# One fused VectorE step for single-row columns of a triangular inverse, late copies and scales on ScalarE, and a new instruction order, in an RWKV-7 and SwiGLU kernel on one core

## The chip, the cores and the metric

The kernel runs on one core of a Trainium2 chip. The metric is the device time of one execution in microseconds (us). Its engines are named as in the profile: PE (TensorE's matmuls; PEld its weight loads), DVE (VectorE), ACT (ScalarE), POOL (GpSimd) and SP (SyncE, which here only issues DMAs). Each engine works off its own list of instructions in order; semaphores tie them together.

## What is computed

An RWKV-7 recurrence over 768 tokens, for 4 batches x 8 heads with 40 numbers a head, and behind it a gated feed-forward block over the 3072 x 320 result:

```
for t in range(S):                                  # r, k, v, w, a, b: (4, 8, 768, 40)
    y[:, :, t] = einsum('bhd,bhde->bhe', rt, state)
    Sa = einsum('bhde,bhe->bhd', state, at)
    state = state * wt[:, :, None, :] - einsum('bhd,bhe->bhde', Sa, bt)
    state = state + einsum('bhd,bhe->bhde', vt, kt)
...
rms = sqrt(mean(x * x, axis=-1, keepdims=True) + 1e-06)   # x: (3072, 320)
xn = x / rms * rms_g
g = xn @ w_gate                                           # (320, 1536)
out = (g * sigmoid(g) * (xn @ w_val)) @ w_out             # (1536, 320)
```

All is in fp32.

## The kernel before

The tokens are cut into 24 chunks of 32. Within a chunk the recurrence is written as matrix products and one triangular inverse for each of the 32 sequences, so that the state moves from chunk to chunk only.

- `front(c)` (line 714) loads a chunk, turns it with TensorE, and forms the decay products, the gram matrices (blocks "gramk") and the triangular factors LT, level by level (1, 2, 4, 8, 16).
- `inverse(c)` (line 823, chunks 4 to 23) inverts the triangular matrix M of every sequence by forward substitution on DVE. Partition p holds a quarter of the rows of one sequence's inverse, so step i has n = i // 4 + 1 rows and m = 31 - i columns. Each of the 31 steps is two instructions of helper line 505: a product into `tmp`, and a subtraction of `tmp` from `Yi`. Chunks 0 to 3 use `early_inverse` (line 841).
- `main(c)` (line 873) does the recurrence proper: products with the state ("state", "lower"), a scaled copy Xs, a second "lower", the copies into VU, the "update" of the state ST; then the scores, the masked scores As for each level, the level products, the output y, its norm, and the turned and scaled columns xg that the feed-forward block reads.
- `feed(g)` (line 1003) takes two chunks (256 tokens) through the feed-forward weights in six pairs of slices: "h64" and "h" blocks of matmuls, Silu on ACT (tile sg), a product on DVE (hT), and "out" blocks that add up in the PSUM tile po.
- `narrow` (line 1039) recodes the weights once at the start.

Helper lines are what the profile shows: 505 every DVE operation, 525 ACT activations, 528 ACT copies, 531 ACT scales, 544 DMAs, 547 matmuls, 550 transposes, 1079 the filler matmul.

None of this is issued as it is recorded. A planner class records every operation as a piece with its dependences. The text `ORDER` then lists the pieces in the order in which they are issued; a number is the distance from the first piece not yet issued, and a "-" is a filler, a 128 x 128 matmul with the identity into an unused part of po that keeps TensorE occupied (line 1079). `PAIRS` gives each of the short-lived PSUM areas ("rooms") one of three PSUM tiles. So the order on each engine is written out by hand, as it were, and is fixed when the kernel is built.

`EARLY, LATE = 4, 6` (line 23) splits the chunks. For chunks from LATE on, four places of `main` use DVE where the chunks before use ACT:

- line 893: of the four copies of the solved block into VU (32 x 320 each), the two with q = 1 go to DVE;
- line 913: the two half copies of the turned r (64 x 512) go to DVE;
- line 929: the masked scores of level 16 are one DVE product of 128 x 512 instead of two ACT scales of 128 x 256;
- line 997: the scaled columns xg are one DVE product of 128 x 384 instead of three ACT scales of 128 x 128.

Of the kernel before, what the change touches and what calls it, by code (L numbers as in the profile page):

```python
# [17 lines left out]
P = 128  # L18
# [4 lines left out]
EARLY, LATE = 4, 6  # L23
# [10 lines left out]
4 5 6 7 8 9 10 11 - - 46 - - - - 43 53 18 - 316 323 58 - - 61 47 60 525 27 44 - - - - 12 13 14 15 16 17 19 317  # L34
- - 313 315 324 314 333 327 328 - 318 325 - 326 - - 73 339 - 74 85 93 84 - 94 82 83 334 337 - 336 335 338 -
340 349 20 21 22 350 355 23 342 343 24 25 26 - 367 - 354 348 - 352 - 344 345 363 346 365 347 - - 351 75 76 362
353 360 628 397 29 - 443 455 - 452 442 36 32 56 - 48 38 59 54 31 441 35 456 - 636 - 451 444 - 62 453 446 33 -
454 - 37 70 45 - 626 445 - 41 638 356 125 122 - 1 332 331 321 103 322 113 114 329 - 95 86 98 379 359 78 79 364
87 361 374 366 - 376 - 378 - - - - 373 77 357 368 371 377 375 387 372 89 88 358 - 461 - 386 369 383 90 80 -
380 381 465 370 466 384 - - 99 463 464 462 470 341 - 91 471 - - 478 - - 481 482 - 385 467 395 468 477 - - 476  # L40
- 483 493 480 - 389 391 390 - - 104 392 81 394 393 105 123 102 472 490 479 627 633 64 42 50 398 448 34 - 623 -
57 67 624 55 - 459 49 634 460 449 52 65 457 51 635 637 - - 473 - 474 491 - 475 450 - - 625 96 492 - 97 396 494
- - 489 - 504 382 100 487 488 - 484 506 - - 399 400 495 401 - 402 403 503 404 - - - 485 496 405 406 407 500
408 409 - 410 505 - 411 - 412 413 414 415 416 507 417 418 497 419 516 420 421 643 422 423 424 - 499 425 426
427 428 - 106 644 - - 502 501 498 107 108 429 124 320 0 317 90 576 - 132 577 - 328 99 643 645 511 510 - 484 -
113 646 644 509 107 - - - - 506 - 507 - 512 658 - 386 650 651 - 663 467 675 - - - 108 116 - 109 662 428 647
516 517 518 515 131 - 521 114 648 124 522 - 657 508 - - - 652 429 578 567 524 - - 61 870 456 861 860 - 640 66
445 430 69 - 598 871 26 - 28 64 639 630 67 629 110 519 520 434 656 - 653 - 654 661 - 117 660 659 127 128 - 655
580 - 115 - - 674 - - 579 513 664 - - - 432 143 431 433 118 525 526 670 568 125 126 669 133 581 666 134 135
435 436 437 438 569 141 142 140 119 687 129 - 668 673 667 161 152 151 163 - 665 144 527 528 529 136 137 138  # L50
679 530 531 532 533 671 534 535 536 537 147 676 160 130 573 571 572 570 672 682 145 146 684 148 538 680 539
540 541 542 543 544 545 546 547 548 149 549 550 685 551 552 553 - 554 582 583 686 - 574 153 555 575 681 156
677 162 139 801 164 678 586 688 167 157 689 - 589 595 590 - 604 693 154 165 155 690 587 588 596 1 0 962 135
145 144 113 146 134 663 519 661 662 560 136 137 143 612 121 122 660 556 557 555 646 554 712 520 664 665 562
129 138 655 147 148 149 563 131 564 568 565 132 569 - 713 566 832 668 33 - 827 841 826 825 - - 837 521 - 835
669 842 828 836 838 0 830 524 522 523 165 521 164 714 656 658 569 138 653 713 669 670 671 - 672 570 673 149
674 571 - 572 675 676 677 678 525 842 526 847 846 843 845 844 - 848 527 153 154 132 162 665 528 715 163 962
139 679 680 150 140 174 141 681 151 682 859 683 684 685 851 849 858 666 852 863 686 687 688 853 717 719 716
718 155 166 156 857 861 689 854 864 690 855 158 691 860 159 856 169 876 157 - 160 850 862 - 692 - 869 722 720
723 - - 546 764 182 - 152 183 185 173 167 547 726 573 168 875 574 - 721 - 575 729 731 865 1009 1008 - 600 -  # L60
1019 599 1018 1016 576 866 693 888 730 735 867 738 737 694 734 732 193 161 184 577 657 175 727 578 728 736 874
695 696 697 868 698 699 871 - 870 739 186 963 733 170 171 - 966 964 - 176 965 177 - 187 873 188 746 745 178
179 740 952 741 742 743 744 - 877 883 879 882 700 194 - - 579 881 880 747 180 872 887 886 172 195 885 580 748
582 - 878 889 891 581 884 749 750 751 752 753 829 590 589 1010 1020 896 754 892 - 890 1026 1013 1027 205 701
202 203 1021 1012 - 1022 - 1023 702 828 1028 705 703 950 951 755 - - 1011 894 893 838 756 1017 0 725 726 576
15 851 850 577 848 772 16 852 849 855 864 17 714 8 - 9 10 18 856 857 578 580 867 - 869 581 525 1093 579 19 23
33 719 720 32 853 723 854 868 862 863 877 866 879 523 717 0 573 515 575 516 713 869 517 847 707 710 711 574 42
0 509 5 839 840 845 841 707 861 567 753 850 14 754 855 856 755 893 568 708 709 569 570 757 853 710 - 711 8 17
851 712 713 714 715 716 717 718 854 719 871 523 21 23 22 867 852 858 756 - 872 - 766 868 524 - 866 869 873 720
# [4 lines left out]
776 876 877 878 18 879 880 881 882 883 884 885 748 - - 871 749 872 - - 1073 944 945 1078 1077 1075 1076 1074  # L74
23 560 719 561 1079 720 562 563 5 6 7 1082 1083 8 - 1090 886 887 1095 1093 1106 1080 947 564 0 12 715 24 - 712
556 13 16 1080 714 23 713 0 878 879 880 0 0 1072 875 1068 709 550 1069 1075 1070 876 1078 1087 877 710 10 1085
11 18 0 1073 1081 1080 9 875 1068 548 549 - - 708 - 1077 709 - 1085 1083 1079 - 929 758 759 876 1086 0 926
1077 17 1087 549 550 22 992 0 15 14 1193 12 542 543 544 765 1239 764 1250 1033 775 1043 867 868 869 1052 750
870 1090 871 872 1082 751 1240 920 1085 752 923 1089 1099 873 1083 874 875 876 1088 9 877 878 879 922 1084 921
545 1079 926 546 880 881 882 0 1085 1079 15 5 18 926 882 0 15 16 5 1079 545 546 1089 928 - 547 - - 548 - - -  # L80
939 1090 882 883 884 8 885 886 887 888 889 890 930 1093 1085 751 1091 929 1094 941 549 551 550 552 937 935 936
18 931 1092 19 891 932 553 938 940 892 893 894 895 896 897 933 898 899 900 942 554 555 1099 1098 1100 9 1101
972 - 0 1170 1083 1084 1085 0 196 546 - 0 0 385 343 344 551 - 386 - 345 552 376 346 - - 387 349 347 415 348
350 354 353 352 351 364 365 390 - 196 195 548 388 549 197 389 553 - 537 554 555 556 557 558 559 560 561 562
563 391 392 393 394 395 - 564 565 566 567 568 569 570 571 572 573 574 575 576 577 396 273 634 637 636 635 0 0
0 0 - 617 393 394 - 0 0 0 615 691 676 463 675 686 680 690 674 687 682 685 684 677 474 571 572 573 574 575 392
576 577 578 579 580 581 582 583 584 585 586 587 588 589 590 591 592 593 464 393 394 395 617 361 362 692 698
396 695 694 - 696 697 693 - - - 398 397 399 758 701 702 712 - 618 400 401 402 616 709 714 594 595 596 597 699
# [339 lines left out]
def kernel(  # L428
# [444 lines left out]
    def main(c):  # L873
# [29 lines left out]
        if c % 2 == 0:  # L903
# [8 lines left out]
            for i in range(2):  # L912
                (copy if c < LATE else dcopy)(R["r2"][half(i)], ps[half(1 - i), i])
# [198 lines left out]
```

## Time and profile before

| | |
|---|---|
| time, median of three runs | 1043.62 us (1041.23 to 1046.06) |
| the profiled execution | 1037.65 us, of which the profile's span is 1035.9 us |
| mean granted PE clock of the profiled execution | 0.972 |
| PE busy, PEld busy | 989.6 us, 807.6 us |
| DVE, ACT, POOL busy | 832.1 us, 450.8 us, 309.1 us |
| DMA queues | 113.03 MB, mean 109 GB/s |

A row of instruction groups reads: helper line, engine, operation, output tile <- input tiles, their shapes, count | busy time of the group in us, mean duration of one in ns | idle time of the engine just before them, and whom it waited for. Busy time is the union of the intervals, so a group of overlapping instructions has less busy time than count times mean. PE's ends are modelled, and a matmul in fp32 leaves two records. A row of a stage gives its start and end, its length, the busy time of PE, PEld, DVE, ACT and POOL with the number of instructions, the granted PE clock, the DMA share and the rate.

### The profile page before, as it was taken

How to read it: one execution, taken by the hardware profiler on the slowest of the kernel's cores; microseconds unless marked ns; L12 is line 12 of the kernel's file. 1: busy time of each engine (PE TensorE's matmuls, PEld its weight loads, DVE VectorE, ACT ScalarE, POOL GpSimd, SP SyncE). 2: the span in 40 equal slices, each digit the busy share in tenths (PEclk: the TensorE clock that was granted, in tenths of full speed). 3: DMA queues.
4: the chain of work that ended last, by engine and by line, in shares of the span. 5: the costliest groups of instructions: out<-in, count | busy, mean ns of one | idle time of the engine just before them, and what ended most of it. 6: DMA issues, size and time to landing. Idle time of an engine off the chain costs nothing.

```text
span 1035.9 us, 56007 instructions
## 1 busy us (share of the span) xinstructions
PE 989.6 (96%) x24842; PEld 807.6 (78%) x24842; DVE 832.1 (80%) x2789; ACT 450.8 (44%) x1019; POOL 309.1 (30%) x554
## 2 busy tenths in 40 slices
PE   7987999999999999999999999999999999999998
PEld 7976877788887787787877787887787877778876
DVE  8987688686869899899989888888799898788410
ACT  5784775543553443443443433452434444341210
POOL 9633413041442233232244232333232432210000
PEclk9976699999999999999999999998999999999999
DMA  8877356755442634434443535334633624422222
GB/s 161 158 194 171 97 158 165 202 131 127 105 87 64 145 79 103 120 65 106 101 98 83 143 75 125 87 68 99 133 62 68 162 65 107 114 51 54 89 77 65
DMA packets 163538, 113.03 MB, mean 109 GB/s; under 512 B 124512, under 2 KB 142880, under 8 KB 163296
## 3 DMA queue, kind: packets, MB, share of 16 engines
q1 hardware_dynamic: 144928, 86.48, 33.8%
q0 software_dynamic: 16192, 22.64, 11.3%
q8 instruction: 195, 3.19, 1.3%
q10 hardware_dynamic: 2176, 0.33, 0.3%
q14 instruction: 47, 0.39, 0.1%
HBM read 93.39 MB, written 15.99 MB: 106 GB/s over the span
## 4 chain that ended last, share of the span: by engine, by line
PE 54%; DVE 30%; issue 5%; DMA 5%; ACT 3%; SPq 2%; POOL 1%; DVEq 0%; ACTq 0%; POOLq 0%
PE ps L547 36%; PE po L547 10%; DVE tmp L505 5%; DVE Yi L505 5%; PE ps L550 5%; DVE LT L505 4%; PE po L1079 3%; DVE K L505 3%; DVE As L505 2%; SPq L544 2%; DVE Ab L505 1%; DVE hT L505 1%; DMA wf<-sW 1%; DVE y L505 1%; DVE T L505 1%
## 5 line engine op out<-in xcount | busy, mean ns | idle before, releaser
L547 PE MATMUL ps<-xg,wf 128*128 128x256 f32 (+1 forms) x1728 | 353.8, 391 | 1.1 <-DMA wf<-sW 0.7
L547 PEld LDWEIGHTS ps<-xg,wf 128*128 128x128 f32 (+1 forms) x1728 | 263.1, 190 | 50.6 <-issue 15.2
L547 PE MATMUL po<-wf,hT 128*128 128x320 f32 x576 | 177.0, 445 | 0.1
L505 DVE TENSOR_TENSOR tmp<-Yi,M 128x60 f32<-128x60 f32 (+24 forms) x620 | 130.3, 210 | 19.8 <-DMA M<-sB 5.4
L505 DVE TENSOR_TENSOR Yi<-Yi,tmp 128x60 f32<-128x60 f32 (+24 forms) x620 | 129.8, 209 | 14.6
L525 ACT ACTIVATE sg<-ps 128x512 f32<-128x512 f32 x72 | 43.0, 597 | 216.5 <-PE ps L547 216.3
L547 PEld LDWEIGHTS po<-wf,hT 128*128 128x128 f32 x576 | 104.6, 191 | 37.0 <-issue 2.1
L544 POOL DMA_DIRECT2D kbn<-in_b_dram x92 | 53.8, 587 | 191.7 <-PE ps L547 169.9
L528 ACT COPY KN<-ps 128x640 f32<-128x640 f32 x96 | 66.3, 692 | 88.0 <-DVE LT L505 50.5
L505 DVE TENSOR_TENSOR K<-K,T 128x512 f32<-128x512 f32 (+1 forms) x192 | 94.0, 496 | 3.4 <-ACT K L528 2.7
L1079 PE MATMUL po<-ident 128*128 128x128 f32 x522 | 92.5, 313 | 3.3 <-DVE po L579 3.3
L505 DVE TENSOR_TENSOR hT<-ps,sg 128x512 f32<-128x512 f32 x72 | 49.6, 689 | 51.6 <-ACT sg L525 51.0
L528 ACT COPY K<-K 128x256 f32<-128x256 f32 (+1 forms) x168 | 72.6, 444 | 35.2 <-DVE K L505 25.0
L547 PEld LDWEIGHTS ps<-Ab,K 40*60 40x60 f32 (+2 forms) x4608 | 68.7, 129 | 19.7 <-issue 6.5
L505 DVE TENSOR_TENSOR As<-ps,msi 128x256 f32<-128x256 f32 (+1 forms) x186 | 82.9, 478 | 1.1 <-PE ps L547 0.6
L547 PE MATMUL ps<-Ab,K 40*60 40x56 f32 (+2 forms) x4608 | 78.2, 217 | 5.2 <-DVE K L505 2.5
L1079 PEld LDWEIGHTS po<-ident 128*128 128x128 f32 x522 | 73.9, 208 | 11.5 <-POOL wan L540 3.3
L544 POOL DMA_DIRECT2D VU<-in_v_dram x92 | 53.8, 586 | 93.5 <-PE ps L550 55.9
L547 PEld LDWEIGHTS ps<-As,KN 128*40 128x40 f32 x3072 | 68.1, 128 | 13.9 <-issue 8.4
L544 POOL DMA_DIRECT2D wn<-in_w_dram x92 | 51.9, 566 | 90.0 <-DVE KN L505 56.4
L547 PE MATMUL ps<-As,KN 128*40 128x32 f32 x3072 | 74.0, 208 | 3.7 <-issue 1.5
L544 POOL DMA_DIRECT2D kbn<-in_k_dram x92 | 53.4, 583 | 76.7 <-PE ps L547 73.3
(137 smaller groups left out, 1470.3 us busy)
## 6 DMA issues: line engine op xcount, KB each, us to landing
wf<-sW SPq DMA_DIRECT2D x82, 480.0 KB, 4.4
M<-sB SPq DMA_DIRECT2D x80, 128.0 KB, 3.6
rn<-in_r_dram SPq DMA_DIRECT2D x24, 160.0 KB, 5.0
out_dram<-o SPq DMA_DIRECT2D x48, 80.0 KB, 3.2
kbn<-in_b_dram POOLq DMA_DIRECT2D x92, 40.0 KB, 3.1
kbn<-in_k_dram POOLq DMA_DIRECT2D x92, 40.0 KB, 3.2
wan<-in_a_dram POOLq DMA_DIRECT2D x46, 80.0 KB, 3.7
wan<-in_w_dram POOLq DMA_DIRECT2D x46, 80.0 KB, 4.3
```

The costliest lines, as they stand in the source:

```text
L505: plan.add("DVE", kind, lambda at: fn(at(o), *m(at)), [o], aps(*args))
L525: plan.add("ACT", "act", lambda at: nc.scalar.activation(at(o), at(a), f, **kw), [o] + aps(acc), [a])
L528: plan.add("ACT", "copy", lambda at: nc.scalar.copy(at(o), at(a)), [o], [a])
L544: plan.add(by, "dma", lambda at: queue.dma_start(out=o, in_=i), [o], [i])
L547: return o, lhsT, rhs, lambda at: nc.tensor.matmul(at(o), lhsT, rhs, start=start, stop=stop, skip_group_check=True)
L550: return o, i, ident, lambda at: nc.tensor.transpose(at(o), i, ident)
L1079: plan.warm = lambda: nc.tensor.matmul(po_[:, 0, DM:DM + P], ident, ident, start=False, stop=False, skip_group_check=True)
```

## The change

A new helper `less` subtracts a scaled row in place with one fused DVE instruction, and `inverse` uses it for the steps with one row (n = 1, so i = 0 to 3). `LATE` is gone: the four places of `main` take the ACT form in all chunks. `ORDER` and `PAIRS` are new texts as a whole; the new order lists 286 fillers and the old one 261.

```
-EARLY, LATE = 4, 6
+EARLY = 4
...
 ORDER = """
-4 5 6 7 8 9 10 11 - - 46 - - - - 43 53 18 - 316 323 58 - - 61 47 60 525 27 44 - - - - 12 13 14 15 16 17 19 317
...
+    def less(o, a, s):
+        dve("stt", lambda out, a, s: nc.vector.scalar_tensor_tensor(out, a, s, out, MUL, SUB, reverse1=True), o, a, s)
+
...
         for i in range(C - 1):
             n, m = i // 4 + 1, C - 1 - i
+            if n == 1:
+                less(Y[:, 0, i + 1:], M[:, i, i + 1:], Y[:, 0, i:i + 1])
+                continue
             tmp = tmp_.next()[:, 0:n * m].rearrange("p (s t) -> p s t", s=n)
...
         for i, q in each_iq:
-            (copy if c < LATE else dcopy if q else copy)(VU[other(i, 4 * q), 4 * q:4 * q + 4, :, 0:D].rearrange("p n o d -> p o n d"),
+            copy(VU[other(i, 4 * q), 4 * q:4 * q + 4, :, 0:D].rearrange("p n o d -> p o n d"),
...
             for i in range(2):
-                (copy if c < LATE else dcopy)(R["r2"][half(i)], ps[half(1 - i), i])
+                copy(R["r2"][half(i)], ps[half(1 - i), i])
...
             G = C // (2 * l)
-            if G == 1 and c < LATE:
+            if G == 1:
                 for i in range(2):
                     scale(As[:, j, :, i], sc.rearrange("p o n t -> p (o n) t")[:, :, 16:C], msi[:, j, i, 0:1])
-            elif G == 1 or l == 1:
-                tt(As[:, j], sc.rearrange("p o n t -> p (o n) t")[:, :, None, 1 if l == 1 else 16:C:2 if l == 1 else 1].to_broadcast((P, NI, 2, 16)),
+            elif l == 1:
+                tt(As[:, j], sc.rearrange("p o n t -> p (o n) t")[:, :, None, 1:C:2].to_broadcast((P, NI, 2, 16)),
                    msi[:, j:j + 1].to_broadcast((P, NI, 2, 16)), MUL)
...
-        if c < LATE:
-            for kt in range(KT):
-                scale(xt[:, :, kt], ps[:, :, kt], gcol[:, kt:kt + 1])
-        else:
-            tt(xt, ps, gcol[:, None, :, None].to_broadcast((P, 2, KT, 64)), MUL)
+        for kt in range(KT):
+            scale(xt[:, :, kt], ps[:, :, kt], gcol[:, kt:kt + 1])
```

More of the change, by code (lines that the diff above doesn't have):

```diff
@@ L39 @@
[L39 to L53, printed above, removed]
@@ L208 @@
[L208 to L209 removed]
[34 rows of a table removed]
[L244 removed]
[8 rows of a table removed]
+- - - 4 5 6 7 18 38 59 - 8 9 53 10 - 317 - - - 43 316 44 525 48 54 318 11 12 13 14 15 16 17 19 - - - - 20 25
+26 21 23 24 - 448 58 - 628 323 313 - - 324 314 328 325 326 315 327 - 93 - 526 445 444 1 74 73 - 322 - 94 83 0
@@ new lines @@
+- 120 - 80 319 331 332 - 335 333 - - 336 - - - 337 348 353 20 340 341 - 365 352 - 53 64 60 25 59 33 449 395
+450 65 58 451 40 69 396 - 338 - 334 347 342 346 350 349 357 440 439 62 - - 27 441 32 26 - 43 47 343 344 - -
+345 - - 351 - 360 363 359 - 73 74 - 75 - - 354 76 361 358 364 355 366 93 362 372 356 371 374 376 375 373 367
+370 369 77 377 78 94 381 96 97 382 383 368 454 598 444 - 34 452 453 - 29 35 37 48 624 455 55 83 82 - 101 - 100
+459 463 462 461 464 - - 460 103 329 330 123 378 - 465 379 393 102 - 112 389 390 387 388 111 - 122 121 392 -
@@ new lines @@
+391 327 328 79 - 476 384 468 - 469 84 87 479 339 466 380 475 492 85 - 86 95 - 480 474 88 481 478 477 385 394
+490 632 44 622 635 625 54 - 28 621 448 633 68 445 - 458 63 - 470 485 - 471 488 487 636 30 623 631 45 457 634
+66 - - - - 447 - 61 - - - - 486 472 - - 473 493 89 98 - 491 - 489 - 502 - 132 576 99 - 90 318 317 577 482 - -
+- 397 398 399 400 497 401 - 483 402 403 404 405 - - - 501 406 407 - 408 503 - 409 505 410 411 - 494 495 412
+498 413 414 415 - - 416 417 - 504 641 - - 418 419 420 - 421 422 423 424 425 426 - 499 - 484 104 500 - 513 - -
@@ new lines @@
+496 - 510 506 642 645 643 646 - - 511 - - 427 - 105 644 428 - 124 106 107 507 509 - - - - 650 467 108 127 651
+658 647 - 648 109 515 518 - - 517 131 - - - 516 - 521 429 110 519 142 520 - 113 125 114 522 115 657 126 578
+652 508 662 656 661 - 116 117 - 663 660 668 118 514 - - 653 - 654 659 655 567 861 49 50 456 70 - 870 38 639
+629 31 640 871 664 430 - - 860 67 630 432 143 431 433 434 - 119 141 - 525 526 128 675 512 129 140 161 163 152
+- 670 581 669 568 133 134 666 579 135 - 671 527 528 680 136 - 137 529 667 138 674 435 436 437 438 569 530 673
@@ new lines @@
+531 532 533 534 535 536 537 672 144 145 146 686 147 538 687 696 - 685 539 540 - 541 665 679 386 542 543 544
+682 151 801 172 162 - 139 130 160 999 573 570 - 571 572 580 676 - 148 149 545 546 547 548 549 550 551 552 677
+153 681 553 683 156 157 691 554 582 583 574 586 180 150 183 171 0 180 574 554 153 154 677 687 590 588 592 -
+688 555 0 - 143 556 551 565 651 661 660 659 658 653 548 549 557 610 558 553 119 134 560 135 645 555 137 138
+655 561 562 566 125 126 127 830 835 825 824 836 839 518 120 710 662 519 563 521 523 663 522 520 826 666 833
@@ new lines @@
+1071 910 - - 736 911 1075 1072 0 0 - - 916 918 1070 530 531 532 949 1076 1078 1077 1075 533 870 912 871 872
+873 874 911 0 874 949 908 875 876 877 878 879 880 918 533 914 916 913 919 920 921 534 535 0 544 545 542 543 -
+346 0 0 345 343 360 361 194 - 544 - 385 386 384 545 626 195 197 196 628 629 627 534 0 1 0 417 343 344 347 345
+346 0 609 610 383 384 543 385 544 545 546 386 387 388 547 548 549 550 551 552 553 554 555 556 557 0 388 389
+390 557 558 559 560 686 687 703 561 562 563 564 565 566 567 708 462 680 668 678 679 671 670 669 685 681 925
@@ new lines @@
+391 471 461 472 684 935 934 924 691 611 689 392 393 688 690 568 569 570 571 - 695 572 696 573 574 575 706 576
+707 718 577 578 579 580 581 582 583 0 0 392 357 610 395 393 394 358 690 396 398 397 691 700 0 698 694 749 611
+581 701 702 612 716 714 610 613 398 399 695 696 582 697 583 584 585 709 586 717 622 404 - - 623 626 706 631
+587 635 710 588 711 723 708 712 634 721 607 707 589 722 630 629 - 713 628 590 591 727 725 592 632 593 594 595
+596 633 405 400 406 401 718 627 407 724 728 726 408 719 638 636 637 730 731 409 410 737 639 720 732 413 640
@@ new lines @@
+657 805 846 849 848 847 - 947 850 981 967 658 968 982 - 659 980 660 979 977 994 851 852 853 435 854 855 978
+984 974 976 436 0 0 646 0 367 368 369 370 711 552 715 554 714 712 551 716 713 553 536 547 548 549 720 550 721
+732 728 - 1 0 0 0 629 630 632 413 414 727 415 729 739 642 553 554 552 555 368 367 369 - 0 0 556 557 554 368
+555 698 699 480 697 689 700 694 703 690 490 953 693 687 688 954 704 944 481 943 414 642 641 415 416 - 643 417
+420 418 419 558 711 559 712 - 428 382 631 738 383 721 736 632 634 633 635 0 719 628 560 561 562 563 564 565
@@ new lines @@
+445 446 447 985 - 440 448 459 623 625 624 622 450 451 - 460 1153 951 701 960 950 700 961 690 1164 841 677 995
+993 991 678 1003 987 779 780 781 782 783 784 785 986 786 787 788 789 790 791 792 793 1000 794 1008 997 998
+1017 795 1006 1001 - 970 796 449 843 845 844 842 1007 1002 1012 797 798 999 1005 848 849 452 846 852 847 799
+861 856 860 1009 800 1010 855 801 859 858 802 803 804 805 453 454 - 1011 853 854 863 865 455 857 806 807 808
+809 810 811 812 813 814 815 816 817 866 461 462 862 864 818 819 820 821 822 823 456 824 867 868 1015 869 873
@@ new lines @@
+825 1004 826 827 828 871 872 870 679 680 1013 683 681 682 463 1019 - 1020 1018 1021 2 1108 1024 1022 1025 1
+1023 829 831 830 832 833 836 834 835 1576 3 1575 0 7 417 418 419 420 421 422 423 424 571 715 491 705 706 697
+501 704 654 - 8 572 573 574 575 576 577 578 579 640 580 581 582 583 584 585 586 587 588 589 710 701 699 714
+492 698 711 708 425 709 700 426 427 652 653 0 0 629 630 632 384 707 419 708 421 709 420 710 711 712 548 385
+422 - 0 0 558 559 711 712 721 421 428 722 579 580 581 727 714 715 582 583 584 585 586 587 588 726 720 589 713
@@ new lines @@
+716 717 590 591 718 592 593 719 - 594 595 596 739 725 597 598 599 600 601 602 603 604 423 422 424 631 - - 605
+425 723 0 631 - 634 737 633 632 429 425 635 723 605 606 607 608 609 610 611 612 730 727 547 734 636 643 770
+732 742 728 750 736 731 - 428 733 644 647 613 839 614 748 729 743 430 735 749 656 615 616 617 431 739 - 426
+744 740 648 649 745 651 654 754 650 741 652 655 653 432 751 - 755 753 756 747 752 441 1 620 3 442 618 450 760
+763 2 490 952 943 658 746 660 953 661 757 758 762 761 765 700 667 690 942 701 - 619 433 659 657 434 666 662
@@ new lines @@
+663 664 668 665 669 670 671 672 673 - 435 766 764 767 621 625 622 624 623 451 955 946 954 945 957 950 691 947
+944 956 960 962 436 967 964 966 965 963 - 437 837 979 438 838 840 768 769 645 646 443 968 674 969 675 771 -
+971 772 773 774 775 972 776 777 - 982 778 779 780 781 977 676 782 783 784 785 786 444 - 983 - 978 439 1163 961
+1153 951 1154 1164 677 678 973 841 445 440 844 845 842 843 446 993 787 788 789 790 791 974 792 980 793 975 794
+795 981 984 996 796 976 797 447 846 847 848 452 985 1028 849 991 989 987 990 995 852 988 798 799 992 - 759
@@ L261 @@
+22001211110022200102022200020112000212110101112100121201202100221122102221112021212021110000102110102200022200
+00011112120111011002220001111021122220020000011020022210111111020212211102221102021221022022020212001100011111
+21101111112211220022220022002112000222000020202021122210011112110120221002200200000000111000021121111201011011
+20222222211020101000022222211220211221110111012001000210210
 """
```

167 lines of the change are left out of this document (65 added, 102 removed), and 203 rows, old and new, of the table ORDER.

## Prediction, made before the changed kernel was run

> **What bounds the kernel now.** I read the page's totals and its slices first, then the busy times of four stages and of one short stretch, then TensorE's (PE's) waits, and last the groups of instructions that the edits touch.
>
> The page: busy time by engine, then the span in 40 slices of 25.9 us, each digit the busy tenths (for PEclk the granted clock).
>
> ```profile
> span 1035.9 us, 56007 instructions
> PE 989.6 (96%) x24842; PEld 807.6 (78%) x24842; DVE 832.1 (80%) x2789; ACT 450.8 (44%) x1019; POOL 309.1 (30%) x554
> PE   7987999999999999999999999999999999999998
> DVE  8987688686869899899989888888799898788410
> PEclk9976699999999999999999999998999999999999
> ```
>
> PE is busy 96% of the span, and from the sixth slice on nearly every digit is 9. VectorE (DVE) follows with 80% and runs at 8 and 9 until the last chunk is done; ScalarE (ACT) has half its time free. The clock digits 7, 6, 6 early on are half-speed stretches that come and go.
>
> Busy time by stage; the columns are length, PE, PEld (weight loads), DVE, ACT and POOL with their instruction counts, granted clock, DMA share, GB/s.
>
> ```profile
> 0.00:130.00 130.00, 111.49 (x2996) 101.39 (x2996) 105.31 (x310) 86.27 (x187) 70.01 (x147) 0.82 0.70 156
> 130.00:208.00 78.00, 71.70 (x1925) 57.84 (x1925) 62.03 (x196) 47.55 (x102) 15.56 (x27) 0.98 0.68 177
> 208.00:962.00 754.00, 736.89 (x19178) 595.26 (x19179) 648.52 (x2251) 305.66 (x709) 222.99 (x380) 1.00 0.43 98
> 962.00:1036.00 74.00, 69.49 (x748) 53.09 (x746) 16.24 (x33) 11.31 (x22) 0.55 (x1) 0.99 0.21 66
> 702.00:728.00 26.00, 23.61 (x554) 19.27 (x553) 19.61 (x81) 5.71 (x13) 11.06 (x19) 0.87 0.58 122
> ```
>
> Nearly all that the change touches lies in the third row. There PE is idle 754.0 - 736.9 = 17.1 us, and the last row shows the one place where the clock falls: 26 us at 0.87 lose 26 x 0.13 = 3.4 us. So 20.5 us is all that better-fed matmuls can win in this stage. DVE is busy 648.5 of 754 us, 86%.
>
> PE's waits from 208 us to the end (who waited for whom: us in all, times, longest); "issue" is a wait that the trace does not name.
>
> ```profile
> PE ps L547 <- issue: 8.8, 10, 2.4
> PE ps L547 <- DVE As L505: 1.0, 3, 0.5
> PE ps L547 <- ACT x L531: 1.0, 1, 1.0
> PE ps L550 <- DVE hT L505: 0.8, 3, 0.4
> ```
>
> Few waits, short ones, and the named ones mostly on DVE. My reading: **PE is the bound from 208 us on, and DVE is close behind**; a lighter DVE can give back part of 20.5 us and no more.
>
> **The change part by part.** First the inverse. Its groups in the trace (busy us, mean ns of one), with the fused form where it stands elsewhere and the shortest step:
>
> ```profile
> L505 DVE TENSOR_TENSOR tmp<-Yi,M 128x31 f32<-128x31 f32 x20 | 3.7, 185 | 5.6 <-DMA M<-sB 5.4
> L505 DVE TENSOR_TENSOR Yi<-Yi,tmp 128x31 f32<-128x31 f32 x20 | 3.8, 190 | 0.5
> L505 DVE TENSOR_TENSOR tmp<-Yi,M 128x30 f32<-128x30 f32 x20 | 3.8, 190 | 0.5
> L505 DVE TENSOR_TENSOR Yi<-Yi,tmp 128x30 f32<-128x30 f32 x20 | 3.8, 189 | 0.6
> L505 DVE TENSOR_TENSOR tmp<-Yi,M 128x29 f32<-128x29 f32 x20 | 3.8, 190 | 0.5
> L505 DVE TENSOR_TENSOR Yi<-Yi,tmp 128x29 f32<-128x29 f32 x20 | 4.0, 198 | 0.5
> L505 DVE TENSOR_TENSOR tmp<-Yi,M 128x28 f32<-128x28 f32 x40 | 7.5, 186 | 1.1
> L505 DVE TENSOR_TENSOR Yi<-Yi,tmp 128x28 f32<-128x28 f32 x40 | 7.4, 185 | 1.0
> L505 DVE TENSOR_TENSOR tmp<-Yi,M 128x8 f32<-128x8 f32 x20 | 3.3, 166 | 0.4
> L505 DVE SCALAR_TENSOR_TENSOR wf<-wf 128x480 f32<-128x480 uint32 x24 | 15.6, 652 | 0.2
> ```
>
> Steps 0 to 3 of each of 20 inverses lose both products and subtractions: 185+190+190+189+190+198+186+185 = 1513 ns a chunk, 30.3 us in all. Four fused steps come instead. The trace has no fused step of 28 to 31 elements. From below its price is that of the shortest step, 166 ns, from above that of the 480-element fused step, 652 ns. The fused row can be split by the slope between 8 and 31 elements, (190 - 166) / 23 = 1.04 ns an element: 652 - 480 x 1.04 = 153 ns fixed, so about 185 ns for 31. I take 195, next to the products of the same width: 4 x 195 = 780 ns a chunk, **a saving of 733 ns, 14.7 us in 20 chunks** (17.0 at 166 ns; a loss of 21.9 at 652). The inverse is a serial chain that other DVE work is threaded through, so it is DVE time that counts, and the two temporaries in turn bind less.
>
> Then the four edits of the main stage for chunks 6 to 23, which take work from DVE to ACT. What goes, and what the same operations cost on ACT in chunks 0 to 5:
>
> ```profile
> L505 DVE COPY VU<-ps 32x320 f32<-32x320 f32 x36 | 17.3, 480 | 6.9 <-ACT VU L528 6.2 <-PE ps L547 0.2
> L505 DVE COPY r<-ps 64x512 f32<-64x512 f32 x18 | 12.4, 689 | 2.6 <-PE ps L550 1.5 <-ACT rE L528 0.7
> L505 DVE TENSOR_TENSOR As<-ps,msi 128x512 f32<-128x512 f32 x42 | 28.5, 684 | 0.0
> L505 DVE TENSOR_TENSOR xg<-ps,gcol 128x384 f32<-128x384 f32 x18 | 9.9, 556 | 6.6 <-PE ps L550 6.6
> L528 ACT COPY VU<-ps 32x320 f32<-32x320 f32 x60 | 25.0, 417 | 23.1 <-PE ps L547 11.7 <-DVE VU L505 10.4
> L528 ACT COPY r<-ps 64x512 f32<-64x512 f32 x6 | 3.5, 580 | 2.5 <-PE ps L550 2.4
> L531 ACT ACTIVATE As<-ps,msi 128x256 f32<-128x256 f32 x12 | 5.5, 471 | 7.2 <-DVE As L505 4.8 <-PE ps L547 2.4
> L531 ACT ACTIVATE xg<-ps,gcol 128x128 f32<-128x128 f32 x18 | 5.7, 387 | 3.9 <-PE ps L550 3.8
> ```
>
> DVE loses 36 x 480 + 18 x 689 + 18 x 684 (the other 24 of the 42 are level 1 and stay) + 18 x 556 = 17.3 + 12.4 + 12.3 + 10.0 = 52.0 us. ACT gains 36 x 417 + 18 x 580 + 36 x 471 + 54 x 387 = 15.0 + 10.4 + 17.0 + 20.9 = 63.3 us. **DVE is 66.7 us lighter in all**: 648.5 becomes about 582 of 754 us, 77% instead of 86%. ACT goes from 305.7 to 369, 49%.
>
> [...]
>
> What do 66.7 us of a second-busiest engine buy? DVE's spare share in the stage goes from 14% to 23%. As an estimate, waits on its queue shrink in the ratio 14 to 23, so of the 20.5 us about 0.4, 8 us, go for that reason; since DVE also gets ahead in the new order (in front of front 6's first gram block both lists hold 120 us of PE work, with 215 us of DVE work in the old and 208 in the new), I take 11 of a possible 20.5, and 0 as the other end. DVE's moves cost nothing there, because PE covers them.
>
> Against it stand two terms. **The feed's boundary**: the last scale of an odd chunk's x comes right before the next feed's first matmul. For the nine feeds from 3 on, three ACT scales in a row, 3 x 387 = 1161 ns, take the place of one DVE product of 556 ns: 605 ns each, 5.4 us at most. The new order lists more PE blocks there than the old at five of the nine, so I take 2. If that cover is gone it is 5.4.
>
> **The fillers.** The order lists dummy matmuls (a "-") where PE is meant to run dry. There are 261 in the old and 286 in the new; behind feed 0's last output block 61 and 79. Their price between 208 and 962 us (two records each):
>
> ```profile
> L1079 PE MATMUL po<-ident 128*128 128x128 f32 x144 | 30.0, 310 | 0.0
> ```
>
> 30.0 / 72 = 0.42 us. Eighteen more cost 7.5 us if PE had work at that point, nothing if it would have waited. I take 2.5.
>
> **The order itself.** Every engine's list is another one. PE's blocks are the same 905, SP's 634 and POOL's 545 pieces too, and no DMA is added. The two orders keep step early on: before feed 0's first matmul the old lists 168 fillers and PE, DVE and ACT work of 44, 124 and 106 us, the new 167 and 44, 120 and 103, and 132 SP pieces against 131. I cost the first 208 us at nothing. The first row above loses 130 x 0.18 = 23 us to the clock there; another pattern of the same stretches could give or take 10. The last row's PE is busy but for 4.5 us and its work is the same: nothing.
>
> **Sum**: -11 + 2 + 2.5 = -6.5 us. The profiled execution took 1037.65 us (its span and 1.75 around it) and would take 1031; it stands 5.97 under the median of the three runs, 1043.62. On the scale of the median: **1037 us**.
>
> **Rivals.**
>
> *ACT gives back what DVE gives.* ACT is a queue, too, and Silu waits in it:
>
> ```profile
> ACT sg L525 <- PE ps L547: 216.3, 59, 14.4
> ```
>
> 59 waits of 3.7 us on the mean, with all that is listed behind them. If the copies that were DVE's now stand there, PE's waits change their name and not their sum; the fused step at its upper price does the same (66.7 - 36.6 = 30 us of relief). For it: ACT work rises by a fifth. Against it: ACT remains idle half the stage. Time: 1043.6, give or take 4.
>
> *Slower: the chain through ACT is exposed.* The place is the recurrence: the second lower matmul, then four copies to VU, then the update. Two copies on each engine took 2 x 480 = 960 ns; four on ACT take 4 x 417 = 1668, 708 ns more, 12.7 us in 18 chunks. With the boundary's 5.4 and the fillers' 7.5 that is 25.6, so 1069; with half of it exposed 1056. It decides once PE has less than 1.7 us listed between those two blocks. Against it: I find 1.9 us and more there in every late chunk of the new order.
>
> *Faster by far: DVE is the true bound.* Then the 66.7 us come through whole: 977. Against it: DVE has 105 us of idle time in the stage, and PE's waits name it for a few us only. [...]
>
> *The clock early on*: plus or minus 10 on a change of nothing, 1034 or 1054.
>
> **How the numbers follow.** Forecast 0.50, its own range 1028 to 1042; ACT gives it back 0.21; exposed chain 0.19; DVE the bound 0.03; the clock 0.07, half each way. A measurement of this kernel tells about 0.5% from no change, so faster is under 1038.4 and slower over 1048.8. Of the forecast 0.40 is faster and 0.10 the same; with the third rival and half the clock's, faster is 0.46. The first rival gives 0.17 to the same and 0.04 to slower: same 0.27, slower 0.04 + 0.19 + 0.04 = 0.27. The range reaches from 1022 (nearly all 20.5 us gone) to 1057 (half the chain exposed); the third rival and the full price of the second stay out.
>
> **What would show it.** DVE's copies to VU and r and its product to xg are gone from the groups, 80 fused steps of Yi at about 195 ns are there, DVE's total is near 765 and ACT's near 514. Right, if PE's idle time from 208 to 962 us falls from 17.1 to about 8 and the first 208 us take as long as before. Wrong, if that idle time stays or grows with waits on ACT's VU or xg (first and second rival), if the stage shrinks by more than PE's idle time (third), or if feed 0 ends at another time.

## The result and the profile after

The changed kernel takes 1089.38 us (median of 4 runs, 1080.70 to 1098.55) against 1043.43 us for the kernel before (4 runs, 1041.23 to 1046.06): a ratio of 1.0412, 95% interval 1.0327 to 1.0496. The prediction was 1037 us, range 1022 to 1057. All ratios, here and below, are of the fast runs alone; here the run of 1098.55 us counts as slow. The profiled execution took 1085.09 us, 47.4 us more than that of before.

The page of the changed kernel: totals, then PE, DVE and the granted clock in 40 slices of 27.1 us.

```profile
span 1083.2 us, 56044 instructions
PE 1011.6 (93%) x24892; PEld 824.8 (76%) x24892; DVE 787.1 (73%) x2619; ACT 504.2 (47%) x1163; POOL 311.1 (29%) x554
PE   7987889998989989999899899999999999999998
DVE  8987778776747877677667678787789689687400
PEclk9967899999989999998989999999999999999999
```

DVE is lighter by 45 us and ACT heavier by 53, as the edits say. But PE's row, an unbroken run of 9s from the sixth slice to the last but one before, is now broken by 8s up to slice 23 (620 us), and more digits of the clock are below 9.

The same stages as before, with a short stretch in the middle of the slow part:

```profile
0.00:130.00 130.00, 108.53 (x2991) 98.88 (x2992) 110.42 (x317) 85.14 (x182) 72.92 (x148) 0.84 0.72 158
130.00:208.00 78.00, 71.70 (x1881) 58.92 (x1882) 60.68 (x193) 47.33 (x106) 15.66 (x28) 0.96 0.64 166
208.00:962.00 754.00, 714.93 (x18117) 575.86 (x18116) 569.27 (x1969) 339.86 (x804) 218.00 (x371) 0.97 0.43 94
500.00:565.00 65.00, 56.86 (x1294) 44.67 (x1296) 41.65 (x142) 23.14 (x53) 18.04 (x31) 0.84 0.46 95
```

The first 208 us look as they did (2996 + 1925 matmul records before, 2991 + 1881 now). From 208 to 962 us PE is idle 39.1 us instead of 17.1, and its clock is 0.97 instead of 1.00, another 754 x 0.03 = 22.6 us. PE gets through 18117 records there instead of 19178. From 500 to 565 us every engine does less than before; the kernel before did this in that stretch:

```profile
500.00:565.00 65.00, 64.09 (x1740) 51.84 (x1738) 58.19 (x197) 26.24 (x62) 25.45 (x44) 1.00 0.31 70
```

What PE waits for, in the changed kernel from 208 us on:

```profile
PE ps L549 <- issue: 17.3, 14, 2.6
PE ps L552 <- issue: 8.3, 4, 3.8
PE po L1081 <- ACT o L530: 5.8, 4, 3.2
PE po L549 <- issue: 3.3, 2, 1.8
PE ps L549 <- DMA wf<-sW: 2.2, 1, 2.2
```

Before, "issue" stood at 8.8 us in 10 waits, and at 1.5 us in one more, a row that the prediction's list passes over:

```profile
PE ps L550 <- issue: 1.5, 1, 1.5
```

These 10.3 us in 11 waits are now 17.3 + 8.3 + 3.3 = 28.9 us in 20. The one engine that is named for more than 0.5 us is ACT with 5.8 us, and there it is fillers (tile po) that wait for its copy of o, four times; before, they did not. Neither ACT's VU nor xg, on which the prediction kept its eye, holds PE up. The longest of the "issue" waits, 3.82 us, in the timeline of PE (start, length, operation, count, [idle before]):

```profile
536.69 1.11 PE L549 MATMUL ps<-xg,wf 64*128 64x256 f32 x8
537.64 0.33 PE L552 MATMUL ps<-ident,kbn 64*104 64x64 f32 x6
541.80 0.65 PE L552 MATMUL ps<-ident,kbn 64*104 64x64 f32 x10 [3.82 <-issue]
542.38 1.19 PE L549 MATMUL ps<-xg,wf 128*128 128x256 f32 x2
```

PE stops **inside** a block: six of sixteen transposes of one tile are done, the other ten read the same tile, and the profile names nothing that they wait for. Between the two halves the trace has a transfer that no line of the kernel issued. The DMA view of 536 to 543 us (queue, kind: packets, MB, share of 16 engines):

```profile
q8 instruction: 1, 0.02, 1.0%
```

It is one packet of the queue that the profile calls instruction, on its way from 539.30 to 540.39 us. PE goes on 1.4 us after its end. The same queue over the whole span, in both kernels alike:

```profile
q8 instruction: 195, 3.19, 1.3%
```

195 packets with 3.19 MB are 16384 bytes each. PE's list in the changed kernel is 50,060 instructions (24,892 matmuls, as many weight loads, 276 others), which is 195.5 x 256; in the kernel before it is 49,972, 195.2 x 256. So **PE's list arrives in pieces of 256 instructions**. The runs below with a longer list bear it out: a_shift128's 50,188 instructions (196.05 pieces) came with 196 packets, a_fill's 50,444 (197.05) with 197. Counting all pauses of over 0.4 us between matmuls after 208 us, by whether PE resumes 1.0 to 2.2 us after the end of such a packet (packets come about every 5 us, 195 of them in 1083.2 us, so that one pause in four or five would do so by chance):

| | pauses, us | of these behind such a packet, us | half-speed clock after 208 us (before 208 us) |
|---|---|---|---|
| before | 15, 13.2 | 10, 10.7 | 6.8 us (51.2) |
| after | 24, 36.9 | 21, 34.3 | 44.4 us (47.8) |

19 of the 21 pauses of the changed kernel, the count of instructions up to them divided by 256, leave 0.75 (the one above: 97.75), and at each of them as many packets have landed as the whole number says (97 at the one above). That is a grid, not chance. They lie between 252 and 786 us, and the wait of 2.2 us that stands against a transfer of wf above is one of them. The other two, 3.2 and 0.4 us, are fillers: they belong to the 5.8 us of waits for ACT's copy of o, and fell behind a packet by chance, as did one of 1.0 us in the kernel before. So the pauses that are piece ends are 19 with 30.6 us, against 9 with 9.7 us before; from here on "at piece ends" means this count.

The half-speed clock of the changed kernel behind 208 us comes in nine stretches of 3.41 to 13.65 us. Each of them begins during a pause of 1.4 to 3.8 us or at most 1.6 us after it: eight at piece ends, and one, of 6.8 us, at the filler's wait of 3.2 us. Other pauses, up to 2.5 us, brought none. At half speed half the time is lost: eight matmuls po<-wf,hT of 128x320 were busy 4.8 us in the stretch of 13.65 us, 0.60 each, and sixteen 5.0 us at the full clock from 430 to 460 us, 0.31 each.

The 47.4 us go: 30.6 - 9.7 = 20.9 to pauses at piece ends, 5.8 to fillers that wait for ACT, 0.5 - 3.5 = -3.0 to all other pauses, (44.4 - 6.8) / 2 = 18.8 to the half-speed clock, 36.5 - 30.0 = 6.5 to fillers (144 records before, 166 after), less (51.2 - 47.8) / 2 = 1.7 for the clock before 208 us: 47.3. Of the clock's 18.8, 3.4 stand behind the filler's wait; so the piece ends cost some 36 us with the clock behind them, and the new fillers some 16. The parts are a count of one trace each and overlap a little, so the sum is closer than they are certain.

### The profile page after: what moved, and what is told of

Its sections match the earlier page's. It is cut to its first block, busy times and chain, and to the rows that moved or that the text cites. A ratio compares the mean times of both kernels' runs of the same rounds, so it can differ in the third digit from the quotient of the medians.

```text
span 1083.2 us, 56044 instructions
## 1 busy us (share of the span) xinstructions
PE 1011.6 (93%) x24892; PEld 824.8 (76%) x24892; DVE 787.1 (73%) x2619; ACT 504.2 (47%) x1163; POOL 311.1 (29%) x554
## 3 DMA queue, kind: packets, MB, share of 16 engines
q8 instruction: 195, 3.19, 1.3%
## 4 chain that ended last, share of the span: by engine, by line
PE 73%; DVE 12%; issue 6%; DMA 4%; ACT 3%; SPq 1%; POOL 1%; DVEq 0%; ACTq 0%; POOLq 0%
PE ps L549 49%; PE po L549 14%; PE ps L552 6%; PE po L1081 4%; DMA wf<-sW 2%; DVE LT L504 2%; DVE tmp L504 2%; DVE Yi L504 1%; DVE K L504 1%; DVE As L504 1%; SPq L546 1%; DMA M<-sB 1%; DVE y L504 1%; DVE Ab L504 1%; DVE vut L504 1%
## 5 line engine op out<-in xcount | busy, mean ns | idle before, releaser
L549 PE MATMUL ps<-xg,wf 128*128 128x256 f32 (+1 forms) x1728 | 366.0, 400 | 10.9 <-issue 5.7
L549 PEld LDWEIGHTS ps<-xg,wf 128*128 128x128 f32 (+1 forms) x1728 | 269.3, 195 | 64.8 <-issue 21.9
L549 PE MATMUL po<-wf,hT 128*128 128x320 f32 x576 | 180.8, 452 | 3.7 <-issue 3.3
L504 DVE TENSOR_TENSOR tmp<-Yi,M 128x54 f32<-128x54 f32 (+1 forms) x540 | 115.3, 214 | 13.5
L504 DVE TENSOR_TENSOR Yi<-Yi,tmp 128x54 f32<-128x54 f32 (+1 forms) x540 | 115.6, 214 | 12.8
L1081 PE MATMUL po<-ident 128*128 128x128 f32 x572 | 101.8, 313 | 9.6 <-ACT o L530 5.8
L1081 PEld LDWEIGHTS po<-ident 128*128 128x128 f32 x572 | 81.8, 209 | 18.4 <-ACT o L530 6.4
L549 PE MATMUL ps<-Ab,K 40*60 40x56 f32 (+2 forms) x4608 | 81.1, 220 | 14.6 <-issue 10.3
L549 PEld LDWEIGHTS ps<-Ab,K 40*60 40x60 f32 (+2 forms) x4608 | 71.2, 131 | 27.1 <-issue 16.1
L530 ACT COPY K<-K 128x256 f32<-128x256 f32 (+1 forms) x168 | 73.4, 445 | 34.5 <-DVE K L504 17.3
L504 DVE TENSOR_TENSOR As<-ps,msi 128x256 f32<-128x256 f32 (+1 forms) x168 | 70.4, 453 | 14.7 <-ACT As L533 5.7
L549 PEld LDWEIGHTS ps<-As,KN 128*40 128x40 f32 x3072 | 64.8, 124 | 13.3 <-issue 10.1
L549 PE MATMUL ps<-As,KN 128*40 128x32 f32 x3072 | 70.8, 204 | 4.2 <-issue 3.9
```

The source lines that it names most:

```text
L504: plan.add("DVE", kind, lambda at: fn(at(o), *m(at)), [o], aps(*args))
L530: plan.add("ACT", "copy", lambda at: nc.scalar.copy(at(o), at(a)), [o], [a])
L549: return o, lhsT, rhs, lambda at: nc.tensor.matmul(at(o), lhsT, rhs, start=start, stop=stop, skip_group_check=True)
L1081: plan.warm = lambda: nc.tensor.matmul(po_[:, 0, DM:DM + P], ident, ident, start=False, stop=False, skip_group_check=True)
```

## The experiments

The first theory, F: the new order puts the ends of PE's 256-instruction pieces into runs of small matmuls, where PE uses up a piece faster than the next one comes, and the pauses pull the clock down. The rivals: the ACT moves (PE waits under another name), and the order as an order (what it lists behind what). The instrument for F is a handful of tiny matmuls into the unused part of po, which move all that follows by a chosen number of instructions on PE's list and nothing else; the output stays the same. One of them is four instructions (two matmul records and their two weight loads; a_fill's 96 lengthen PE's list from 50,060 to 50,444).

**Shift the old kernel by 96 and by 256 instructions, the new one by 128** (24, 64 and 32 tiny matmuls at the start of the list):

```
     def issue(self):
...
+        for _ in range(24):
+            self.shift()
...
+    plan.shift = lambda: nc.tensor.matmul(po_[0:32, 0, DM:DM + 16], ident[0:32, 0:32], ident[0:32, 0:16], start=False, stop=False, skip_group_check=True)
```

> The kernel before with 24 tiny matmuls (32 x 32 by 16 columns, into the unused part of po) ahead of PE's list, 96 PE instructions; all else is unchanged. Theory F (fetch): PE's instructions come in pieces of 256, and PE runs dry where the end of a piece falls into a run of small matmuls; in the traces 10 such gaps cost 10.7 us after 208 us in the kernel before, 21 cost 34.3 us in the changed one, all at the same place modulo 256. Moving the list by 96 puts the ends elsewhere, where by the block times of the trace about twice as much time is short: 1080 to 1110 us. Theory A (ScalarE's longer queue made the changed kernel slow) and theory O (its order lists work too late): nothing is moved but 24 short matmuls, 1043 to 1047.

> The kernel before with 64 of the same tiny matmuls, 256 PE instructions, a whole piece. Theory F: the ends fall where they fell, so 1043 to 1050, the fillers' own time beside it. Theories A and O: 1043 to 1050 too. It is the control for the run with 96: if this one is as slow, it is the fillers and not the place.

> The changed kernel with 32 of the tiny matmuls, 128 PE instructions. Theory F: the ends move by half a piece, and by the trace's block times somewhat less is short there, about 10 us less of gaps and fewer half-speed stretches: 1060 to 1085 instead of 1089. Theories A and O: 1089 to 1092.

Measured, against 1041.28 us for the kernel before on the same chip: b_shift96 1098.86 us (1.0512, 1.0452 to 1.0573); b_shift256 1051.93 (1.0074, 1.0028 to 1.0120); a_shift128 1074.15 (1.0304, 1.0243 to 1.0365). The first and the third lie where F expected them. But for 24 tiny matmuls at the start, nothing differs between the first and the kernel before except the place of the piece ends, and it is as slow as the changed kernel. Its page, stage and waits of PE from 208 us on:

```profile
span 1099.1 us, 56103 instructions
PEclk9976799899999999899999998999899999999999
...
208.00:962.00 754.00, 711.79 (x18083) 571.71 (x18082) 613.14 (x2119) 297.38 (x686) 218.34 (x372) 0.97 0.42 97
...
PE ps L549 <- issue: 31.7, 22, 5.0
PE ps L552 <- issue: 5.3, 5, 2.6
```

It has the changed kernel's signature without any of its edits: idle 42.2 us, clock 0.97, "issue" 37.0 us. The shift by a whole piece gives nearly all of it back; what is left, 0.7% or 8 us by the ratio, is a little over what was expected, and as an estimate 64 x 8.7 / 96 = 5.8 us of it are the tiny matmuls themselves (their price is from a_fill below). Its stage and its largest wait:

```profile
208.00:962.00 754.00, 735.44 (x19052) 594.12 (x19052) 648.25 (x2250) 305.00 (x707) 222.39 (x379) 1.00 0.43 98
...
PE ps L549 <- issue: 10.8, 13, 2.7
```

More added work, 2.7 times as many tiny matmuls, and 47 us less time: it is the phase that counts, that is, where in the list the pieces end, and it repeats after 256. In the changed kernel the shift lowers the ratio from 1.0412 to 1.0304, some 11 us, with intervals that overlap a little (pauses at piece ends 26.1 us instead of 30.6, 27.3 us at half speed instead of 44.4).

**Two more phases of the old kernel**, 160 and 240 (40 and 60 tiny matmuls), tell whether the worst lies between and the best at 0:

> The kernel before with 40 of the tiny matmuls ahead, 160 PE instructions. Theory F: the place of the ends decides, and it repeats after 256; by the block times of the trace of before this place is nearly as bad as 96 (84 us of blocks short of 4.3 us against 91 there and 44 where they stand): 1080 to 1102. If the 55 us of the run with 96 were chance: near 1045.

> The same with 60, 240 PE instructions: 16 short of a whole piece, 55 us of short blocks by the same sum. Theory F: between the control with 256 (1052) and the bad places, 1052 to 1068, though it has more fillers than the run with 160. If the slowdown grew with the number of fillers: over 1100.

Measured against 1050.50 us: b_shift160 1105.71 (1.0531, 1.0450 to 1.0612); b_shift240 1059.51 (1.0106, 1.0037 to 1.0176). The first is 3.7 us over what was expected, the second within it. Pauses at piece ends by shift: 9.7 us at 0, 37.1 at 96, 35.4 at 160, 19.3 at 240, 11.5 at 256. The old order stands at the best phase found. The 4.3 us under which the expectations count a block as short are the author's estimate, and no run shows them as a limit: in the kernel before, the nine pieces that ended in a pause took 1.9 to 5.2 us, the pause not counted, and 94 others that took no longer than 5.2 passed without one.

**Put the piece ends of the new kernel right**, by 96 tiny matmuls at 16 places in the feeds (a word "+" in ORDER):

```
 for word in ORDER.split():
...
+            if word == "+":
+                self.shift()
+                continue
```

> The changed kernel with 96 tiny matmuls (384 PE instructions) put at 16 places in the feeds from feed 0 on, so that the ends of the 256-instruction pieces fall beside the runs of small matmuls; nothing else is moved, and the work on PE grows by some 5 to 10 us. Theory F: gaps at the ends fall from 34 to about 15 us and half-speed stretches with them, 1055 to 1075. Theories A and O: more work and nothing gained, 1092 to 1100.

Measured: 1066.18 us (1064.69 to 1071.14) against 1047.05, ratio 1.02 (1.0134 to 1.0266), below the interval of the change and where F expected it: some 22 us better by the ratios, with more work in it. Its stage, one wait of PE and two groups (the tiny matmuls are L1083, two records each):

```profile
208.00:962.00 754.00, 732.07 (x19006) 592.51 (x19008) 594.96 (x2063) 355.70 (x843) 221.67 (x377) 1.00 0.44 98
...
PE ps L550 <- issue: 11.5, 12, 2.2
...
L1083 PE MATMUL po<-ident 32*32 32x16 f32 x192 | 8.7, 179 | 1.5 <-issue 1.5
L1082 PE MATMUL po<-ident 128*128 128x128 f32 x572 | 102.7, 315 | 9.1 <-ACT o L531 5.8 <-DVE po L582 3.3
```

Pauses at piece ends are back at 12.1 us and the clock at 1.00, from 30.6 and 0.97. What is left against before is the remedy, luck and the new fillers: 8.7 us of tiny matmuls; 64.9 us at half speed in the first 208 us against 51.2, half of which, 7 us, is lost; 5.8 us of fillers that wait for ACT's copy of o, as in the changed kernel; and 8.5 us more of fillers than before from 208 to 962 us (38.5 against 30.0). DVE is lighter here too, with 595 of 754 us busy instead of 648.5, and no gain from it shows.

**All edits in the old order**, the pieces renumbered:

> All edits of the change, but in the order and the rooms of the kernel before: each fused step stands where its subtraction stood, the scales on ScalarE where the one product stood. PE's list is that of before but for 8 waits fewer. Theory F: the ends fall nearly where they fell, 1033 to 1048, with DVE 60 us lighter. Theory A: the chain through ScalarE is what costs, 1070 to 1090. Theory O: the old order is not to blame, 1033 to 1048.

Measured: 1082.06 us, ratio 1.0384 (1.0318 to 1.0451). What theory F expected was missed by 34 us; the 1070 to 1090 of theory A, by which the moves to ACT cost, was met. Pauses at piece ends are as before (8, 8.2 us), and yet it is as slow as the change. PE's waits from 208 us on:

```profile
PE ps L545 <- ACT xg L529: 7.9, 4, 3.3
PE ps L545 <- issue: 7.4, 7, 2.8
PE ps L545 <- ACT KN L526: 7.1, 5, 4.0
PE ps L548 <- ACT xg L529: 4.6, 3, 2.7
```

In the old order it is the rival that costs: PE waits 12.5 us for xg and 7.1 for KN on ACT, and loses another 15 us to the clock (37.5 us at half speed against 6.8). So there are two costs, one for each order, and the edits had to be taken apart.

**The parts alone, in the old order**: the fused steps (only `less` and its use in `inverse`), the moves to ACT (only the other four edits), the moves without xg.

> The kernel before with the fused steps of the inverse alone, each where its subtraction stood; main and the order of all else are those of before. PE's list is unchanged to the instruction. Theory F (fetch): 1036 to 1044, DVE 15 us lighter and the piece ends where they were. Theory A (the moves to ScalarE cost in an order that was not made for them): the same, for no move is made. A rival on the fused step itself: if it is slow (652 ns), up to 1065.

> The four moves to ScalarE alone, in the order of the kernel before. With both edits this order took 1082 us, with 11.6 us of gaps at the piece ends (before: 10.7) and about 29 us of other PE gaps. Theory A: the moves alone bring these other gaps, 1078 to 1092. If the fused steps caused them instead: 1040 to 1050.

> The moves to ScalarE in the old order, without the one of the feed's columns xg, which stays one DVE product. With it this order took 1087 us, and 12.5 us of PE's named waits were for ScalarE's xg in the run with all edits, 4.2 for VU and 7.1 for KN. If the boundary of the feed is the place: 1055 to 1070. If ScalarE's queue as a whole is too full for this order: 1075 to 1087.

In moves_no_xg the last of the four edits reads:

```
-        if c < LATE:
+        if c < 6:
             for kt in range(KT):
                 scale(xt[:, :, kt], ps[:, :, kt], gcol[:, kt:kt + 1])
         else:
             tt(xt, ps, gcol[:, None, :, None].to_broadcast((P, 2, KT, 64)), MUL)
```

| | this / before, same chip | ratio (95%) |
|---|---|---|
| fused_old_order | 1041.50 (12 runs) / 1047.05 (17 runs) | 0.9940 (0.9907 to 0.9973) |
| moves_old_order | 1086.82 / 1047.05 | 1.0371 (1.0313 to 1.0428) |
| moves_no_xg | 1059.62 / 1050.50 | 1.0114 (1.0039 to 1.0190) |

All three came out within what the theory that they bear out expected. The fused steps alone are 0.6% faster than the kernel before; pauses at piece ends are 7.2 us there instead of 9.7, and how much of the gain is the lighter DVE's is not shown. The moves alone cost 3.7%, some 39 us, and without xg 1.1%, some 12: with the three scales at the feed's boundary go about 27 of the 39. PE's waits in moves_old_order:

```profile
PE ps L549 <- issue: 10.9, 11, 3.1
PE ps L549 <- ACT xg L533: 7.9, 4, 3.3
PE ps L549 <- ACT KN L530: 7.1, 5, 4.0
PE ps L552 <- ACT xg L533: 4.6, 3, 2.7
```

and in moves_no_xg, where the xg rows are gone and KN's stays:

```profile
PE ps L547 <- ACT KN L528: 7.1, 5, 4.0
PE ps L547 <- issue: 4.9, 8, 1.1
```

12.5 us of waits for xg are gone with some 27 us of time. The clock behind 208 us ran 17.1 us at half speed instead of 44.4, which is 13.7 us of time; but pauses at piece ends fell too, from 11.0 to 4.0 us, so the 27 us are not xg's alone.

**The new order with the old instructions**:

> The code of before in the order and the rooms of the change: the pairs of steps stand where the fused ones stood, the one product on DVE where the last of ScalarE's scales stood. Theory F: the gaps at the piece ends come with the order of PE's blocks, 1075 to 1100. If it was the edits that cost in any order: 1040 to 1055. Theory O without F (the new order lists work too late for a lighter DVE only) would show it slow as well, but with PE's gaps elsewhere than at the ends.

Measured: 1177.22 us against 1047.05, 1.124 (1.1166 to 1.1313), 77 us beyond what theory F expected. Its largest waits of PE from 208 us on:

```profile
PE ps L544 <- issue: 14.6, 11, 3.0
PE ps L547 <- DVE xg L502: 12.5, 5, 4.6
PE ps L547 <- ACT VU L525: 12.4, 5, 7.4
PE ps L547 <- DVE r L502: 6.1, 4, 4.4
```

The new order does not fit the old instructions: with xg and r still on DVE, PE waits for them. An order is written for one set of durations. By the waits, the new order does take away what the moves cost in the old one. On F the trace says more than the time: 19 of its pauses, 29.7 us, lie on the grid of piece ends. So the pauses at piece ends go with the order and not with the instructions: 9.7 us (kernel before) and 8.2 (edits_old_order) in the old order, 29.7 and 30.6 (changed kernel) in the new one.

What is shown and what not: that the place of the piece ends alone moves this kernel by some 55 us, and that this repeats after 256 to within 0.7%, is shown by the shifts; that the changed kernel loses 30.6 us at such ends is in its trace, and moving the ends takes back 22 us in a_fill; the 11 us of a_shift128 are within what the intervals leave open. That its half-speed stretches come from pauses is argued: each begins at one, and they go together in all these kernels (6.8 us at half speed in b_shift256 and a_fill, 44.4 in after and b_shift96). Open is when the end of a piece stops PE: the 256 instructions ahead of a pause took 1.8 to 3.6 us, the pause not counted, where a piece of the changed kernel behind 208 us takes 5.5 on the mean, pauses counted; but 16 pieces that were as short passed without a pause. Other traffic may play a part, which no run varied: in its 19 pieces that ended in a pause the other DMA queues kept the 16 engines 0.66 busy up to the pause, in those 16 that did not 0.28. Whether the change in an order with good piece ends would beat the kernel before was not tried without added work.

## Why the prediction was wrong

The step that failed is **"The order itself"**: "PE's blocks are the same 905 ... and no DMA is added ... I cost the first 208 us at nothing", and behind 208 us the order had no term at all. The same blocks in another sequence have the piece ends at other places. The term left out measured 20.9 us of pauses at piece ends and 15.4 of the clock behind them; the other 3.4 of the clock, and 5.8 us of waits, are new waits of fillers.

The door to it was the reading of PE's waits. The prediction took "issue" for "a wait that the trace does not name" and added it to the 20.5 us that a lighter DVE could win. A third view of the same trace, the DMA view's instruction queue, names most of it: 9.7 of the 13.2 us of pauses over 0.4 us before were piece ends, which a lighter DVE does not shorten. Of these pauses only 3.5 us, waits on DVE and ACT among them, were for sale.

Point by point:

- **PE is the bound from 208 us on**: right. DVE fell by 79 us in that stage, from 648.5 to 569.3 (part of it because less work was done there), and nothing came of it; in a_fill, with the pauses back at 12.1 us, neither. The rival by which DVE is the true bound, 977 us, is gone with it.
- **The fused step**: predicted 195 ns between 166 and 652, measured 245 to 247. Two of the four rows in the changed kernel's groups:

```profile
L519 DVE SCALAR_TENSOR_TENSOR Yi<-M,Yi 128x31 f32<-128x31 f32 x20 | 4.9, 245 | 2.2 <-DMA M<-sB 1.1 <-DMA sY<-Yi 0.7 <-issue 0.4
L519 DVE SCALAR_TENSOR_TENSOR Yi<-M,Yi 128x28 f32<-128x28 f32 x20 | 4.9, 247 | 0.6
```

  Four take 986 ns, so a chunk saves 527 and not 733 ns, 10.5 us in all. The sizing split the 652 ns of the long fused row by the products' slope, which left 153 ns fixed; by the two fused rows themselves, as an estimate, the slope is (652 - 245) / 449 = 0.91 ns an element and 217 ns are fixed. The long row takes a constant as its factor and the new steps one number per partition; whether that matters was not tried.
- **The moves**: right in each price but xg's, 369 ns where 387 was taken. The rows of the moved operations, all on ACT now, with the shared level-1 product left on DVE:

```profile
L530 ACT COPY VU<-ps 32x320 f32<-32x320 f32 x96 | 40.0, 416 | 27.8 <-PE ps L549 26.2
L533 ACT ACTIVATE xg<-ps,gcol 128x128 f32<-128x128 f32 x72 | 22.7, 369 | 26.6 <-PE ps L552 21.4 <-DVE Yi L504 5.2
L533 ACT ACTIVATE As<-ps,msi 128x256 f32<-128x256 f32 x48 | 21.4, 471 | 36.7 <-DVE As L504 29.6 <-PE ps L549 7.1
L530 ACT COPY r<-ps 64x512 f32<-64x512 f32 x24 | 13.9, 580 | 10.1 <-PE ps L552 9.7
L504 DVE TENSOR_TENSOR As<-ps,msi 128x512 f32<-128x512 f32 x24 | 16.4, 682 | 2.2 <-PE ps L549 1.4 <-ACT As L533 0.9
```

  ACT's total came to 504.2 (predicted 514), DVE's to 787.1 (predicted 765). The durations of all DVE instructions, added up, fell by 60 us (963.8 to 903.7), close to 10.5 + 52.0; DVE's busy time, the union of the intervals, fell by 45, since neighbours on DVE overlap (before, 963.8 us added up are 832.1 busy; after, 903.7 are 787.1). The prediction took durations off a union.
- **Relief of 11 us**: not there. What PE waited for was mostly not DVE. In the old order the fused steps alone gained 5.6 us by the medians.
- **The feed's boundary, 2 us, at most 5.4**: for the new order right as far as the waits go, since no wait on xg is among PE's. For the old order, wrong by far: 12.5 us of waits, and some 27 us of time with all that goes with them. The bound of 605 ns a feed counted three scales against one product; the longest wait for xg was 3.3 us. That the scales stand in ACT's list behind other work is the likely reason, which was not tried alone.
- **The fillers, 2.5 us, at most 7.5**: 6.5 more us of them between 208 and 962 us, and 5.8 us in which fillers themselves waited for ACT's copy of o, which is new: a filler writes into po, too, and has to wait until o is out of it. With the 3.4 us of clock behind the longest of these waits, fillers cost some 16 us, where the prediction's bound was 7.5.
- **The first 208 us at nothing**: right within the 10 left for the clock (feed 0's last product out at 229.8 us, 225.9 before).
- **The exposed chain through ACT**, at 1056 to 1069 the rival nearest to the result, is not what happened: PE's one wait on VU is 0.4 us.

## What to carry to other kernels

Where TensorE is the bound and its list is long, look in the trace for pauses inside a block of small matmuls and for the packets of the instruction queue beside them, and price any reordering, or any change in the number of matmuls, with the phase of the list: shifting it by a few tiny matmuls is a cheap test, and moved this kernel by some 55 us. A wait that the profile puts down to "issue" need not be slack that a lighter engine can win; most of it was not here (9.7 of its 10.3 us in the kernel before were piece ends). Test an edit apart from the new order that comes with it: here the fused steps gain 0.6% alone, inside a change that loses 4.1%, and the new order with its own edits is no faster than the old order with them (1.0412 and 1.0384).

## What the runs showed of the hardware

- Ends of 256-instruction pieces stopped PE for 0.4 to 3.8 us each in the two kernels, where the list was short on time: in the changed kernel the 256 instructions before a pause took 2.6 us on the mean, the pause not counted, against 5.5 for all pieces, pauses counted. 137 of its 156 pieces behind 208 us ended in no pause of over 0.4 us.
- In the changed kernel behind 208 us half-speed stretches lasted 3.41 us or a multiple of it, up to 13.65: nine of them, eight at pauses of 1.4 to 3.2 us, shorter than the shortest stretch, and one at 3.8.
- A fused step with a factor per partition, 28 to 31 elements wide, took 245 to 247 ns in the changed kernel, where a plain product of that width took 185 to 190 in the kernel before.
